# Replanning the instruction order of an attention and gated-convolution kernel, and moving part of the last batch's output behind its branch

## The chip, the cores and the metric

The kernel runs on one core of a Trainium2 chip. The metric is the device time of one execution in microseconds (us). An engine's program is a list of instructions that it takes strictly in order; engines wait for each other through semaphores. The names used here are those of the profile: PE is the matrix engine (PEld its weight loads), DVE the vector engine, ACT the scalar engine, POOL the GpSimd engine, SP the engine that issues most transfers.

## What is computed

For 8 batches, 12 heads, 448 positions and 64 channels a head:

```python
scores = scale * np.matmul(q, k.transpose(0, 1, 3, 2))
e = np.exp(scores - m)                       # m: row maximum
attn = e / (np.sum(e, -1, keepdims=True) + np.exp(-m) + 1e-09)
x = np.matmul(attn, v)                       # heads side by side: (8, 448, 768)
x1, x2, x3 = split(x @ w_proj, 3)            # w_proj: (768, 2304)
x2_conv = irfft(rfft(x2, axis=1) * rfft(filter_fft, axis=0), n=448, axis=1)
out = (x1 * x2_conv * x3) @ w_out            # (8, 448, 768), float32
```

## The kernel before, in words

The work of a batch has two halves. **Attention** runs over 6 pairs of heads (`attention(i)`, i from 0 to 47): PE makes scores (L817, L819), ACT exponentials (L830, L836), PE the product with v and the sums (L848, L856), DVE divides (L869 to L871) into the tile `xb`, which is turned into `xT` by PE (L953) or by a transposing transfer (L944). The exponentials are taken without the row maximum; the smallest denominators are collected in `low`, and at the end `watch()` makes a flag of them. **Dense** (`dense(b)`) folds `xT` on DVE (L1017, L1022), projects to x2 (`P`, L1045; `PS`, L1067, for batches 5 to 7), goes to the spectrum (`Z`, L1115 or L1119), multiplies it by the filter's on DVE (L1133, L1139), goes back (`I`, L1204), unfolds on DVE (L1222, L1224, L1233), makes the gates x1 and x3 (`G`, L1165, ACT L1177, DVE L1180), multiplies (L1248, tiles `yT` and `yR`), and projects out (`O`, L981), which ACT copies out of PSUM (L1279) and SP stores (L1286, L1289).

q, k and v come in float32. Those of batches 0 and 1 are staged (`staged`), and those of batches 2 to 7 loaded through rooms (`loaded`); SP issues the loads, and POOL casts them to bf16 (L468, L474, L481 and L597, L599, L613, L634, L646). The weights are loaded by POOL, which casts them on the way: the filter (L711 to L715), `wproj_bf` in four pieces (L795) and `wout_bf` (L800).

**The order is made by a planner.** `Plan.add` takes tasks: an engine, a cost in us, a wanted time, what it needs and makes, what buffers and PSUM banks it takes and gives back, and for a transfer its own duration (`dma`). `Plan.run` plays them through: whenever an engine is free it takes, among the first 160 of its tasks by wanted time, the first that is ready by the planner's own clock. The order found is then written out, and is fixed: on the chip an engine waits in that order. The wanted times come from lists of constants (`ATT`, `SLOT`, `LATER` for the pairs, `DENSE`, `PACE`, `FOLD`, `GATE`, `OUT` for the dense work, `LEAD`, `HOLD`, `EARLY1` for loads, `LOAD` for weights). They are priorities, and only an argument `after` forbids an earlier start; the weights' `LOAD` times are such bounds. `Plan.fillers` puts small matmuls on a tile of zeros (L1431) into the planned idle time of PE from 3 to 36 us.

**The end.** After `plan.run()` each engine loads the flag into a register (L1488) and compares (L1490). If a denominator was too small, the body of the branch does everything again in a stable way; with these inputs it isn't run. Tasks added with `keep=True` are not written out in their place but by `plan.rest()` (L1509), behind the branch, because the body would otherwise have to undo them. In the kernel before, these are the copies and stores of the last batch's output tiles of `st` 2 and 3 (four copies at L1279, three stores); all its matmuls and the copies of `st` 0 and 1 stand ahead of the branch:

```python
keep = b + 1 == n_batches and st > 1
```

The last batch takes its output tiles (st, ch) in the order (0,0), (0,1), (1,0), (1,1), (3,0), (3,1), (2,0), (2,1); the first three are multiplied in two parts (4 and 2 of the 6 matmuls).

Of the kernel before, what the change touches and what calls it, by code (L numbers as in the profile page):

```python
# [20 lines left out]
SP = 112  # L21
# [20 lines left out]
class Plan:  # L42
# [12 lines left out]
    DELAY = 0.8  # L55
    TURN_ISSUE, TURN_HOLD = 1.2, 0.3
    SHIFT = {}
    OPEN = 8
    BEGIN = 0.75

# [13 lines left out]
    def add(self, eng, cost, want, emit, need=(), make=(), take=(), give=(), dma=0.0, run=256, n=1, after=0.0, begun=(), late=0.0, turn=False, part=None, keep=False):  # L74
        want += self.SHIFT.get(part, 0.0)
        self.tasks.append((want, len(self.tasks), eng, cost, emit, need, make, take, give, dma, after, run, n, begun, late, turn, keep))

    def run(self):
# [14 lines left out]
        free = {e: self.BEGIN for e in queue}  # L93
        begin = {}
# [103 lines left out]
        while any(queue.values()):  # L198
            moved = False
            for e in queue:  # L200
# [18 lines left out]
                end = free[e] = now + t[3]  # L219
# [4 lines left out]
                if t[9]:  # L224
                    q = queues["POOL" if e == "POOL" else "SP"]
                    if t[15]:

                        begin[t[1]], free[e] = now, 1e9
                    q.append([now + 1.1 if t[15] else end + self.DELAY, t[9], t])
                    q.sort(key=lambda h: h[0])  # L230
                else:
                    done(t, end, e)
# [12 lines left out]
        for i, (_, t) in enumerate(order):  # L245
            if i in full:
                self.fill(*full[i])
            if t[16]:
                mine = {x for key in t[8] for x in self.banks.get(key, ())}
                assert not any(mine & {*self.banks.get(key, ())} for _, o in order[i:] for key in o[7])  # L250
                self.kept.append(t)
            else:
                t[4]()
# [30 lines left out]
def kernel(  # L284
# [14 lines left out]
    NSTAGED = 2  # L299
    TURNED = (5, 6, 7)  # L300
    SPIN = 38
    EARLY1 = -37.75
    ATT = [-28.66, -4.15, 82.66, 88.63, -11.62, 245.08, 188.29, 237.93]
    SLOT = [1.03, 11.04, 13.5, 24.02, 22.71, 6.32, -1.86, -14.05]
    LATER = [6.49, 7.1, 16.33, 26.04, 24.32, 5.99, -1.3, -2.41]
    GATE = [0.05, 3.09, 0.39, 0.33, 5.25, -4.56, -17.89, 14.82]
    OUT = [-3.82, -5.82, 1.94, 3.86, -0.16, 42.73, -1.71, 0.08]
    DENSE = [90.41, 90.02, 159.62, 189.84, 206.75, 232.76, 314.84, 367.32]
    PACE = [1.11, 3.24, 3.53, 2.89, 4.16, 2.12, 4.12, 4.66]
    FOLD = [-97.25, -48.09, -37.96, -86.97, -68.61, 36.98, -3.27, -113.82]  # L310
    BPS = -32.54
    RE1 = -1.35
    WT = -57.72
    FT = -26.69
    LEAD = [[-7.64, -155.36, 10.87, 83.2, 24.35, -314.59, 11.65], [-160.72, 35.85, -106.91, 64.9, -12.51, -20.99, -13.36], [-43.31, 108.31, -186.99, -24.09, -295.49, 10.18, 192.79], [-246.92, 212.51, -116.13, -76.77, -135.16, -81.28, 61.49], [-160.4, -105.54, 47.21, 18.57, 50.04, -291.15, -125.18], [-84.91, -13.51, -157.96, 191.73, -71.67, 188.48, 135.6]]
    LOADS = ((1, 0), (1, 1), ("F", None), (0, None), (2, None), ("O", None))
    LOAD = [8.53, 39.59, -42.24, 14.08, 48.04, 64.38]
    XALL = (1, 2, 3, 4, 5, 6, 7)
    HOLD = [16.92, -20.63]
    FOLD0 = [-27.94, 10.52, -65.43]  # L320
# [104 lines left out]
    def staged(b):  # L425
# [3 lines left out]
        for hp in range(NHP):  # L429
# [6 lines left out]
            for n, (name, x, at, size) in enumerate(parts):  # L436
                src = stage(g, at, size)

                def load(name=name, x=x, src=src, hp=hp, g=g):
# [13 lines left out]
                add("ACT" if first else "SP", 0.52 if first else 0.3, -21.0 if first else want + 0.1 * n, load, need=need,  # L453
                    make=[("s" + name, g)], after=hold, dma=(0.98 if name == "q" else 0.76) if b == 0 else 0.88 if name == "q" else 0.68, run=57,
                    begun=[("i" + name, g)])
                if hp == 0 and name != "q":
                    add("SP", 0.3, want + (0.05 if name == "k" else SLOT[0] + 0.05) if b == 0 else want - RE1 + 0.1 * n,
                        lambda name=name, x=x: nc.sync.dma_start(rests[:, "kv".index(name)], shared(x, b)),
                        need=[("cr" + name, b - 1)] if b else (), make=[("r" + name, b)],
                        dma=0.95, run=15, begun=[("ir", b)])  # L460
# [25 lines left out]
                if name == "v":  # L486
                    add("POOL", 0.72, tau(g) + (1.0 if b == 0 else -4.0), cast,
                        need=[("sv", g)] + ([("V", old, 1)] if b >= 2 else []), make=[("cv", g), ("v", g)])
                else:
                    add("POOL" if on_pool else "DVE", 0.65 if on_pool else 0.42, tau(g) - 5.0, cast,  # L490
                        need=[("s" + name, g)] + ([("c" + name, g - 1)] if g else []), make=[("c" + name, g)], take=[(name + "0", g)])
            if hp == 0:
                for u in range(2):
                    c = slice(64 * u, 64 * u + 64)
                    on_pool = b > 0 or u == 1
                    add("POOL" if on_pool else "DVE", 0.55 if on_pool else 0.37, tau(g) - 5.9 if g else 3.0,
                        lambda c=c, on_pool=on_pool: (nc.gpsimd if on_pool else nc.vector).tensor_copy(
# [71 lines left out]
    def loaded(b):  # L569
# [21 lines left out]
        for n, (name, x) in enumerate((("k", k), ("v", v))):  # L591
            add("SP", 0.3, tau(i0) - lead[0] - 0.2 + 0.1 * n,
                lambda name=name, x=x: nc.sync.dma_start(rests[:, "kv".index(name)], shared(x, b)),
                need=[("cr" + name, b - 1)], make=[("r" + name, b)], dma=0.85, run=15)
        for u in range(2):
            c = slice(64 * u, 64 * u + 64)
            add("POOL", 0.6, tau(i0) - lead[1] - 0.2, lambda c=c: nc.gpsimd.tensor_copy(kn[c, :, 0, c], rests[c, 0]),  # L597
                need=[("rk", b)] + (["zero kn"] if b == NSTAGED else [("kT", i) for i in range(i0 - NHP, i0)]), make=[("crk", b)])
        add("POOL", 0.56, tau(i0) - lead[3], lambda: nc.gpsimd.tensor_copy(vn[b % 2][:, :, 3, 0:DH], rests[:, 1]),  # L599
            need=[("rv", b), ("V", i0 - NHP - 1, 1)], make=[("crv", b), ("vr", b)])  # L600

        for hp in range(NHP):
# [3 lines left out]
            add("SP", 0.3, tau(g) - lead[4],  # L606
# [4 lines left out]
                need=[("cq", g - QS)] if n >= QS else staged_done, make=[("sq", g)], dma=0.88, run=57)  # L611
            add("POOL", 0.65, tau(g) - lead[5],
# [5 lines left out]
            if hp % few == 0:  # L618
                gs = range(g, g + few)
                add("SP", 1.3, tau(g) - lead[6], lambda hp=hp: q_turn(hp), need=[("cq", i) for i in gs] + [last],  # L620
                    make=[("qT", i) for i in gs], dma=(0.72, 1.9)[few > 1], run=11, late=-0.7, turn=True)
            for n, (name, x) in enumerate((("k", k), ("v", v))):
# [5 lines left out]
                add("SP", 0.3, tau(g) - lead[0] + 0.1 * n,  # L628
                    lambda x=x, hp=hp, src=src: nc.sync.dma_start(src.rearrange("p (u c) -> p u c", u=2), rows(x, b, hp)),
                    need=room, make=[("s" + name, g)], dma=0.68, run=57)  # L630
                sv = src.rearrange("p (u j d) -> p u j d", u=2, j=3)
                if name == "k":
                    add("POOL", 0.6, tau(g) - lead[1],
# [4 lines left out]
                    if hp % few == 0:  # L638
                        gs = range(g, g + few)
                        add("SP", 1.3, tau(g) - lead[2], lambda hp=hp: k_turn(hp), need=[("ck", i) for i in gs] + [("crk", b), last],  # L640
                            make=[("kT", i) for i in gs], dma=(0.97, 2.05)[few > 1], run=11, late=-0.7, turn=True)
                else:
# [5 lines left out]
                    add("POOL", 0.72, tau(g) - lead[3], cast, need=[("sv", g), ("V", g - 2 * NHP, 1)], make=[("cv", g), ("v", g)])  # L648
# [156 lines left out]
    def attention(i):  # L805
# [161 lines left out]
        if b in XALL or b > 1 and hp < NHP - 1:  # L967
            if hp in (2, NHP - 1 if b in XALL else NHP - 2):
                ps = range(0, 3) if hp == 2 else range(3, hp + 1)
                add("SP", 1.3, w, x_dma, need=[("xb", NHP * b + h) for h in ps] + old,  # L970
                    make=[m for h in ps for m in (("X", NHP * b + h), ("xT", b, h))], dma=(0.0, 1.1, 1.7, 2.1)[len(ps)], run=11, late=-0.7, turn=True)
# [17 lines left out]
    def dense(b, calm=True):  # L989
# [39 lines left out]
        for ds in (slice(0, 3), slice(3, 6)) if b else (slice(0, 3), slice(3, 4), slice(4, 6)):  # L1029
# [3 lines left out]
            for n in range(2):  # L1033
                add("DVE", (0.65, 0.54)[n] * slow, w, lambda ds=ds, n=n: first(ds, n),
                    need=[("xT", b, h) for h in range(ds.start, ds.stop)] + ([("fold", b, g, 0)] if n else []),
                    make=[("fold", b, g, n)], take=[("uw"[n], (b, g))])
                for pg in (2 * n, 2 * n + 1):
                    add("DVE", 0.26 * slow, w, lambda ds=ds, pg=pg: second(ds, pg),
# [51 lines left out]
        def PS(dt):  # L1090
# [7 lines left out]
            if dt % 3 == 2:  # L1098
                add("SP", 1.3, w - 2.0, lambda: turn2(ch), need=[("x2s", b, d) for d in range(dt - 2, dt + 1)],
                    make=[("x2", b, pg, ch) for pg in range(4)], take=[("x2", b)], give=[("x2s", b)],  # L1100
                    dma=2.1, run=11, late=-0.7, turn=True)
# [42 lines left out]
        def Z(par, ch):  # L1144
# [9 lines left out]
            for n in range(2):  # L1154
                tk = (f"t{n}", (b, par, ch))
                add("DVE", 0.48, w + 1.0, lambda n=n: product(par, ch, n),
                    need=[("xs", b, par, ch), ("hrs", par)], make=[("t", b, par, ch, n)],
                    take=[tk], give=[xs])
                add("DVE", 0.28, w + 1.5, lambda n=n: total(par, ch, n), need=[("t", b, par, ch, n)],
# [90 lines left out]
        def I(dt):  # L1250
# [9 lines left out]
            for n in range(2):  # L1260
                add("DVE", 0.32, w + 0.4, lambda n=n: halves(dp, n), need=[("cr", b, dp)], make=[("cw", b, dp)],
                    take=[cw], give=[cr])
            for n in range(2):
                add("DVE", 0.31, w + 0.5, lambda n=n: unfold(dp, n), need=[("cw", b, dp)], make=[("cv", b, dp)],
                    take=[cv], give=[cw])
            for n in range(2):
                add("DVE", (0.48, 0.15)[n], w + 1.0, lambda n=n: gated(dp, n), need=[("cv", b, dp), ("g", b, dp)],
# [23 lines left out]
        def O(st, ch):  # L1291
            hy, os_ = hold(("O", b, st, ch)), ("os", (b, st))
            keep = b + 1 == n_batches and st > 1
            if keep:
                plan.open.append((st, ch))
# [3 lines left out]
            if 2 * st + ch < 3:  # L1299
# [4 lines left out]
                    make=[("O", b, st, ch)], give=[mem_])  # L1304
            else:
                add("PE", 0.98, w, lambda: project(st, ch, None, hy), need=need + ["wout"], make=[("O", b, st, ch)],
                    take=[hy], give=[mem_])
# [232 lines left out]
```

## Time and profile before

| | |
|---|---|
| median of 3 runs (lowest, highest) | 390.51 us (389.07, 391.35) |
| the profiled execution, its own time | 387.02 us |
| its span, from first to last instruction | 385.2 us |
| granted clock of PE, mean | 0.997 |
| busy: PE, PEld, DVE, ACT, POOL | 364.6, 225.9, 262.2, 264.0, 114.2 us |
| PE: instructions | 3694 matmuls, as many weight loads |
| moved by DMA; read from and written to HBM | 66.82 MB; 43.86 and 11.01 MB |

The span leaves out 1.8 us that lie around the instructions. Busy time counts each moment once for an engine; PE's includes the small matmuls on zeros. The profile's groups give, for a line of the program, the engine, the operation, the tiles, how often, the busy time, the mean duration in ns, and the idle time of the engine just ahead with what ended it. An arrow `<-DVE xb L871` reads "released by that instruction".

### The profile page before, as it was taken

To read this page: it belongs to the slowest core of one execution; us is meant where nothing else is said; L and a number is where in the kernel's file an instruction comes from. 1 tells how busy PE (TensorE), PEld (TensorE's weight loads), DVE (VectorE), ACT (ScalarE), POOL (GpSimd) and SP (SyncE) were. 2 spreads that over 40 slices of the span, in tenths; PEclk is the share of its full clock that TensorE was granted. 3 is DMA by queue.
4 is the path that set the end of the run, shared out by engine and by line. 5 is a ranking of instruction groups with operands and counts; after the bars stand their busy time and mean duration, and the time that the engine had idled before them with its cause. 6 is when DMAs were issued, how large, how long until landed. Compare 5 with 4: busy or idle time off the path is not lost. (4 is left out here: it accounts for less than half of the span.)

```text
span 385.2 us, 9574 instructions
## 1 busy us (share of the span) xinstructions
PE 364.6 (95%) x3694; PEld 225.9 (59%) x3694; DVE 262.2 (68%) x677; ACT 264.0 (69%) x457; POOL 114.2 (30%) x240
## 2 busy tenths in 40 slices
PE   8888899999998999999998999999999999999992
PEld 6666575557664666556754675655555555555651
DVE  6484778875789547886599784675397833968650
ACT  6668776874877768778758468866788776446531
POOL 4925816030652445434367324110000000000000
PEclk9999999999999999999999999999999999999998
DMA  8999999977989699999998983594522164223214
GB/s 212 258 223 246 228 229 222 177 160 225 220 210 249 188 275 256 234 205 281 246 262 180 268 216 103 148 172 128 85 42 43 43 163 125 43 39 85 82 41 129
DMA packets 125744, 66.82 MB, mean 173 GB/s; under 512 B 82493, under 2 KB 122112, under 8 KB 125696
## 3 DMA queue, kind: packets, MB, share of 16 engines
q1 hardware_dynamic: 120976, 60.54, 67.6%
q0 software_dynamic: 4480, 5.41, 8.3%
q8 instruction: 30, 0.49, 0.5%
q10 hardware_dynamic: 240, 0.23, 0.2%
q14 instruction: 18, 0.15, 0.1%
HBM read 43.86 MB, written 11.01 MB: 142 GB/s over the span
## 5 line engine op out<-in xcount | busy, mean ns | idle before, releaser
L830 ACT ACTIVATE e<-psum 128x896 bf16<-128x896 f32 x144 | 127.1, 923 | 21.3 <-PE psum L817 20.8
L1165 PE MATMUL psum<-xT,wproj_bf 128*128 128x448 bf16 x576 | 121.4, 352 | 0.4 <-DVE g L1180 0.4
L1165 PEld LDWEIGHTS <-wproj_bf 128*128 128x128 bf16 x576 | 54.2, 97 | 45.2 <-issue 2.0
L981 PE MATMUL psum<-wout_bf,yT 128*128 128x384 bf16 x288 | 52.1, 326 | 0.0
L856 PE MATMUL psum<-vn,e 128*128 128x65 bf16 x1152 | 44.9, 194 | 0.0
L817 PE MATMUL psum<-qT,kT 64*128 64x448 bf16 x288 | 41.5, 355 | 3.2 <-DVE xb L871 2.1
L1045 PE MATMUL psum<-wproj_bf,xf 128*113 128x384 bf16 x240 | 43.1, 327 | 0.2 <-DVE xb L871 0.2
L1177 ACT CAST x<-psum 128x448 bf16<-128x448 f32 x48 | 25.7, 536 | 24.7 <-PE psum L1165 23.1
L856 PEld LDWEIGHTS <-e 128*128 128x128 bf16 x1152 | 40.2, 97 | 3.2
L1279 ACT COPY osb<-psum 128x384 f32<-128x384 f32 x56 | 25.7, 487 | 21.8 <-PE psum L981 18.0
L869 DVE TENSOR_SCALAR den<-psum 128x8 f32<-128x8 f32 x48 | 7.8, 162 | 48.2 <-PE psum L856 48.0
L1133 DVE TENSOR_TENSOR t<-xs,hrs 113x768 bf16<-113x768 bf16 (+1 forms) x64 | 36.8, 607 | 2.5 <-ACT xs L1127 2.4
L981 PEld LDWEIGHTS <-yT 128*128 128x128 bf16 x288 | 27.2, 98 | 18.9 <-issue 1.4
L613 POOL CAST nat<-nat 112x512 bf16<-112x512 f32 x36 | 26.9, 755 | 34.6 <-DMA nat<-in_q_dram 34.1
L1045 PEld LDWEIGHTS <-xf 128*113 128x113 bf16 x240 | 31.0, 132 | 8.8 <-issue 1.1
L871 DVE TENSOR_TENSOR xb<-psum,den 128x512 bf16<-128x512 f32 x48 | 33.2, 691 | 1.7
L1180 DVE TENSOR_TENSOR g<-x,psum 128x448 bf16<-128x448 bf16 x48 | 29.5, 615 | 6.0 <-PE psum L1165 6.0
L836 ACT ACTIVATE er<-psum 128x448 bf16<-128x448 f32 x48 | 26.3, 548 | 9.1 <-PE psum L819 9.1
L646 POOL CAST vn<-nat 128x192 bf16<-128x192 f32 x58 | 22.3, 408 | 34.2 <-DMA nat<-in_v_dram 18.0
L1127 ACT CAST xs<-psum 113x384 bf16<-113x384 f32 (+1 forms) x64 | 28.2, 497 | 5.4 <-PE psum L1119 2.1
L1213 ACT CAST cr<-psum 128x452 bf16<-128x452 f32 x48 | 25.0, 549 | 7.3 <-PE psum L1204 7.0
L817 PEld LDWEIGHTS <-kT 64*128 64x128 bf16 x288 | 9.1, 94 | 26.4 <-issue 23.9
(125 smaller groups left out, 474.5 us busy)
## 6 DMA issues: line engine op xcount, KB each, us to landing
nat<-in_q_dram SPq DMA_DIRECT2D x47, 224.0 KB, 4.5
out_dram<-osb SPq DMA_DIRECT2D x24, 384.0 KB, 3.0
nat<-in_k_dram SPq DMA_DIRECT2D x41, 192.0 KB, 4.3
nat<-in_v_dram SPq DMA_DIRECT2D x41, 192.0 KB, 4.6
wproj_bf<-in_moe_w_proj_dram POOLq DMA_DIRECT2D x2, 1152.0 KB, 15.0
rests<-in_k_dram SPq DMA_DIRECT2D x8, 192.0 KB, 5.1
rests<-in_v_dram SPq DMA_DIRECT2D x8, 192.0 KB, 5.0
out_dram<-osb SPq DMA_DIRECT2D x8, 192.0 KB, 3.1
```

Of the source, the lines that this page charges most:

```text
L613: lambda hp=hp, qsrc=qsrc: nc.gpsimd.tensor_copy(qn[:, hp].rearrange("p j (u d) -> p u j d", u=2), qsrc.rearrange("p (u j d) -> p u j d", ...
L817: nc.tensor.matmul(sc[:, u, 0:S], kT[b % 2][c, hp, t, :], qT[b % 2][c, hp, :])
L830: nc.scalar.activation(to, of, AF.Exp, scale=SCALE)
L836: nc.scalar.activation(to, of, AF.Exp, scale=SCALE)
L856: nc.tensor.matmul(out_bank(u)[:, n, :], P["e"][1 + t][:, u * S + n * 128 : u * S + n * 128 + 128], vn[b % 2][:, hp, 4 * u + t, :], start= ...
L871: nc.vector.tensor_tensor(W["xb", b][:, hp].rearrange("p n (u d) -> p u n d", u=2), op[:, :, :, 0:DH], rec[:].unsqueeze(3).to_broadcast([1 ...
L981: nc.tensor.matmul(ops[:n, :DCH], y[:, dt, 0:n], wout_bf[:, dt, ch * DCH : (ch + 1) * DCH], start=(dt == 0), stop=(dt == NDT - 1),)
L1045: nc.tensor.matmul(pps[:FQ, :DCH], W["xf", b][:, pg, kt, 0:FQ], wproj_bf[:, kt, D + ch * DCH : D + (ch + 1) * DCH], start=(kt == 0), stop= ...
L1127: nc.scalar.copy(L["xs", par, ch][:K, pg % 2, :], L["Z", pg, ch][:K, :DCH])
L1133: nc.vector.tensor_tensor(t[:K], L["xs", par, ch][:K], h, op=ALU.mult)
L1165: nc.tensor.matmul(p[:, :S], wproj_bf[:, kt, 2 * part * D + dt * 128 : 2 * part * D + (dt + 1) * 128], xT()[:, kt, 0:S], start=(kt == 0), ...
L1180: nc.vector.tensor_tensor(g[:, dt, :], L["x1", dt], p[:, :S], op=ALU.mult)
```

## The change

Three things are changed. None alters what is multiplied or how often, apart from the matmuls on zeros, whose number follows from the plan.

1. **The planner's model.** A shared port is added: a task with `port=True` (the bf16 sums and products on DVE: L1014 to L1022, L1133, L1139, L1222 to L1248, and the casts on DVE) and every task of POOL that isn't a transfer may not overlap by more than 0.16 us with one of the other engine. The casts on POOL get lower costs of their own. An issue on SP costs 0.5 instead of 0.3, and a transfer begins 1.15 (SP) or 1.9 us (POOL) after its issue starts. Durations and shares of transfers are changed a little.
2. **The constants** of the wanted times are all new, so that the whole order is new. Two pieces of `wproj_bf` get later bounds: the first half of the x2 part from 8.53 to 22.57, the x1 part from 14.08 to 21.47.
3. **The end.** All copies and stores of the last batch's output go behind the branch, and so do the matmuls of its tiles (1,1), (3,0), (3,1), (2,0), (2,1). Those of `TAIL` stay ahead of it. If the branch were taken, the body would multiply the `TAIL` tiles again.

```diff
-    DELAY = 0.8
-    TURN_ISSUE, TURN_HOLD = 1.2, 0.3
+    DELAY = (1.15, 1.9)
+    TURN_ISSUE, TURN_HOLD = 1.4, 0.4
+    PORT = 0.16
...
-                end = free[e] = now + t[3]
+                end = now + t[3]
+                if t[17]:
+                    end = max(now, port["POOL" if e == "DVE" else "DVE"] - self.PORT) + t[3]
+                    port[e] = end
+                free[e] = end
...
-                    q.append([now + 1.1 if t[15] else end + self.DELAY, t[9], t])
+                    q.append([now + self.DELAY[e == "POOL"], t[9], t])
...
+    TAIL = ((0, 0), (0, 1), (1, 0))
...
-    EARLY1 = -37.75
-    ATT = [-28.66, -4.15, 82.66, 88.63, -11.62, 245.08, 188.29, 237.93]
-    SLOT = [1.03, 11.04, 13.5, 24.02, 22.71, 6.32, -1.86, -14.05]
-    LATER = [6.49, 7.1, 16.33, 26.04, 24.32, 5.99, -1.3, -2.41]
...
-    DENSE = [90.41, 90.02, 159.62, 189.84, 206.75, 232.76, 314.84, 367.32]
+    EARLY1 = -43.88
+    ATT = [-15.23, -18.02, 73.57, 108.86, 36.32, 226.98, 200.24, 223.07]
+    SLOT = [8.8, 12.52, 11.4, 17.9, 3.71, 0.09, -13.77, -15.9]
+    LATER = [5.59, 20.08, 17.05, 19.3, 12.65, -6.44, -8.83, 0.12]
...
+    DENSE = [84.12, 91.93, 155.59, 189.18, 196.52, 273.03, 309.83, 339.74]
...
     LOADS = ((1, 0), (1, 1), ("F", None), (0, None), (2, None), ("O", None))
-    LOAD = [8.53, 39.59, -42.24, 14.08, 48.04, 64.38]
+    LOAD = [22.57, 41.98, -44.36, 21.47, 43.35, 63.54]
...
-                add("SP", 0.3, tau(g) - lead[0] + 0.1 * n,
+                add("SP", 0.5, tau(g) - lead[0] + 0.1 * n,
...
-                    add("POOL", 0.6, tau(g) - lead[1],
+                    add("POOL", 0.47, tau(g) - lead[1],
...
-                add("DVE", 0.48, w + 1.0, lambda n=n: product(par, ch, n),
+                add("DVE", 0.48, w + 1.0, lambda n=n: product(par, ch, n), port=True,
...
-            keep = b + 1 == n_batches and st > 1
-            if keep:
+            keep = b + 1 == n_batches
+            last = keep and (st, ch) not in TAIL
+            if keep and not last:
                 plan.open.append((st, ch))
...
-                    take=[hy], give=[mem_])
+                    take=[hy], give=[mem_], keep=last)
             add("ACT", 0.38, w, lambda: project_back(st, ch), need=[("O", b, st, ch)], make=[("os", b, st)],
                 take=[os_], give=[hy], keep=keep)
...
+        y, yr = W["yT", n_batches - 1], W["yR", (n_batches - 1) // 2]
         W.clear()
         main = plan
         for b in range(n_batches):
+            W["yT", b], W["yR", b // 2] = y, yr
```

## The prediction on record

> **What bounds the kernel now.** I read the page's busy times and slices first, then stretches of the span, then the pauses of PE, then the end in order of time.
>
> ```profile
> PE 364.6 (95%) x3694; PEld 225.9 (59%) x3694; DVE 262.2 (68%) x677; ACT 264.0 (69%) x457; POOL 114.2 (30%) x240
> ...
> PE   8888899999998999999998999999999999999992
> ```
>
> PE is the bound: busy 95%, and in the slices short only in the first four or five and in the last. So the change can gain in three places alone: the start, the few pauses between, the end. The stretches say how much lies in each.
>
> ```profile
> 7.75:40.00 32.25, 26.80 (x418) 19.54 (x418) 18.43 (x53) 23.73 (x38) 19.88 (x50) 1.00 1.15 244
> ...
> 40.00:370.00 330.00, 322.87 (x3144) 195.48 (x3144) 236.33 (x598) 232.86 (x406) 91.19 (x179) 1.00 0.75 169
> ```
>
> After the time, the columns are PE, PEld, DVE, ACT, POOL. **Start:** 7.75 us is where the first exponential begins. PE looks busy for 26.80 of 32.25 us, but 7.03 are matmuls on zeros (L1431 in the same stretch), so it works some 19.8. ACT idles 32.25 - 23.73 = 8.5 us; attention, all that PE has there, can't pass it. **Middle:** PE idles 330 - 322.87 = 7.1 us. From 280 to 320 and 330 to 370 it doesn't pause.
>
> **Part 1, casts and products apart.** The group of L1233 in two windows, 40 to 260 us (POOL casts) and 260 to 386 (POOL does next to nothing):
>
> ```profile
> L871 DVE TENSOR_TENSOR xb<-psum,den 128x512 bf16<-128x512 f32 x30 | 20.7, 691 | 1.0
> ...
> L1233 DVE TENSOR_TENSOR cv<-cw 128x448 bf16<-128x448 bf16 x30 | 13.1, 474 | 0.5
> ```
>
> ```profile
> L871 DVE TENSOR_TENSOR xb<-psum,den 128x512 bf16<-128x512 f32 x12 | 8.3, 691 | 0.4
> L1233 DVE TENSOR_TENSOR cv<-cw 128x448 bf16<-128x448 bf16 x18 | 6.2, 388 | 0.3
> ```
>
> The bf16 sum takes 474 ns beside casts and 388 without; the product out of PSUM takes 691 in both. So what the planner now keeps apart does collide. The same difference over the other bf16 forms of 40 to 260 us: L1233 30 x 86 = 2.6 us, L1133 20 x 107 + 20 x 69 = 3.5, L1139 20 x 89 + 20 x 87 = 3.5, L1022 18 x 83 + 18 x 28 = 2.0, L1248 15 x 31 + 14 x 95 = 1.8, L1222 15 x 51 = 0.8: 14.2 us of DVE. But DVE idles a third of the span, so this counts only where PE waits for it. One such place, in order of time:
>
> ```profile
> 207.15 0.87 DVE L1233 TENSOR_TENSOR cv<-cw 128x448 bf16<-128x448 bf16 x2
> ...
> 207.66 1.39 POOL L613 CAST nat<-nat 112x512 bf16<-112x512 f32 x2 [0.18 <-DMA nat<-in_q_dram]
> ...
> 208.05 0.51 DVE L1248 TENSOR_TENSOR yR<-g,cv 128x128 bf16<-128x128 bf16 x1
> ...
> 208.91 0.69 DVE L871 TENSOR_TENSOR xb<-psum,den 128x512 bf16<-128x512 f32 x1
> ...
> 209.66 0.37 PE L1204 MATMUL psum<-bt,yh 113*128 113x113 bf16 x4 [1.41 <-DVE xb L871]
> ```
>
> Beside POOL's casts the small product takes 0.51 us (220 ns without casts), the division behind it is late, and PE waits 1.41 for it. PE's longer pauses after 40 us (from one matmul's start to the next, less the usual spacing) sum to 9.0; three have a product drawn out by a cast ahead of them, at 161.9, 195.9 and 207.9 us: 0.58 + 0.99 + 1.58 = 3.15. Four more (81.9, 123.3, 124.5, 233.3: 0.90 + 0.80 + 0.57 + 1.08) are mostly the order's own, scores put right behind the matmuls whose division frees their banks. A new order can lose as much as it wins in such places: between a loss of 3 and a gain of 3.15 + half of 3.35 I take a gain of **1.3**, some 40% of what the collisions cost.
>
> Longer issues on SP (0.5 for 0.3) alter the plan alone: load issues on the chip take 0.37 to 0.46 us at the least and in the median (L446). Casts on POOL average 570 (L634) and 755 ns (L613) with collisions, so 0.47 and 0.58 beside a port are no gain in themselves. I put both at nothing, behind 70% idle POOL; if the cover is gone, they show as waits of PE on casts, in the range.
>
> **Part 2, the start.** Weights now come no earlier than 21.47 and 22.57 in planned time, where POOL issued them at 15.15 and 16.57. From 20 to 30 us POOL's queue moved 1.47 MB and SP's 0.72, so the weights slow the loads of batches 0 and 1: q, k, v issued then landed after 10 to 13 us, against 4.3 to 4.6 over the whole run. The filter, which isn't moved, fills POOL's queue until about 19 us, and the weights flow from 20. With about 2 us from issue to first packet they would flow from 23.4: 3.4 us in which SP's queue gets some 230 KB/us instead of 75, or 0.5 MB, which is two or three loads. The two pieces are 1152 + 576 KB, at 147 KB/us 11.8 us, landed by about 35; the first use of the x2 part is at 42.4 (L1045). So they are still in time. What is late next is ACT: it also makes the filter's copies there (29.05 to 33.96 us, 4.2 us of work), so pair 5 starts at 33.87 whatever the loads do. Of ACT's 8.5 us the named waits on PE are nearly all; recovering 2 us of ACT gives PE 2 x 19.8 / 23.73 = 1.7. Bounds: a loss of 5.0 (late weights, below), a gain of half of the 8.5, 4.2 x 0.83 = 3.5. I take a gain of **1.5**.
>
> **Part 3, the end.** Before:
>
> ```profile
> 376.34 2.11 PE L981 MATMUL psum<-wout_bf,yT 128*128 128x384 bf16 x12
> 378.63 1.63 ACT L1279 COPY osb<-psum 128x384 f32<-128x384 f32 x4 [3.56 <-PEq L1490]
> 379.51 1.12 SPq L1289 DMA_DIRECT2D out_dram<-osb  x2
> 380.75 0.52 SPq L1286 DMA_DIRECT2D out_dram<-osb  x1
> ```
>
> Four copies and three issues stand behind PE's end: its last matmul starts at 378.13, the last store is issued at 380.75, 2.62 us later. After, seven copies (0.37 us apart) run beside the 30 matmuls behind the branch (30 x 0.162 = 4.9 us), and only one is left when PE ends. By the unhindered tile at 372.97, a copy starts 0.04 behind its last matmul's end: 0.33 + 0.04 + 0.49 + 0.02 = 0.88 to the store. Gain 2.62 - 0.88 = 1.74. What it adds is a stop of PE in the middle of its output tiles:
>
> ```profile
> L1488 PEldq TENSOR_LOAD <-flag x1: 488/488/488, 375.4 to 375.4; - x1
> ...
> L1490 PEldq COMPARE_BRANCH  x1: 488/488/488, 376.0 to 376.0; - x1
> ...
> L1490 PEldq EVENT_SEMAPHORE  x1: 51/51/51, 378.5 to 378.5; - x1
> ```
>
> PE's sequencer reads the flag and branches while some 2.7 us of matmuls are still queued, and the semaphore step behind the branch waits for the last of them (378.45). The next matmul could start at about 378.8 instead of 0.162 behind the last, 378.29: 0.5 lost. Bounds: 0.3 (semaphore at once) and 3.1 (375.4 to 378.5, nothing hidden). Queued behind it are 30 matmuls, and all copies and stores wait for them; SP no longer waits at the branch for the output stores (it did, until 377.84), which wins nothing as PE was last. Net **1.2**; the last store, alone in the queues, may also land up to 0.5 earlier (2.74 against 3.26 us), which I leave in the range.
>
> A rule speaks against this part: the Trainium skill (Runtime: NRT & Kernel Launch, Instruction fetch mechanics) says that a taken branch to a target outside the fetched window stalls until a page is fetched. Here PE stood behind the branch at 376.47 and was ready by 378.50, so the row allows up to 2.0 us of fetch, which the queue of matmuls hid; by the row I charge 0.5, by the rule unhidden 3.1.
>
> **Sum:** 1.3 + 1.5 + 1.2 = 4.0 us. Against the profiled execution 387.02 - 4.0 = 383.0. The runs shown have a median 3.5 us above it; the same gain from 390.51 gives **386.5**.
>
> **Rivals.**
> - Only the end counts: the new order makes as many pauses as it removes. For it: every wait of an in-order engine that goes uncovers another. 390.51 - 1.2 = 389.3. 0.14.
> - More comes out: half of ACT's idle start (3.5), all collisions (3.15), the end with its landing (1.6), 8.25 in all: 382.3. For it: PE never pauses after 280 us, so all won earlier is kept. 0.16.
> - The fetch isn't hidden: 3.1 lost instead of 0.5, 386.5 + 2.6 = 389.1. Against it: in the rows above the branch ran ahead. 0.06.
> - Slower: the weights come late. If they move only as POOL's queue did from 10 to 20 us (0.72 MB in 10 us), 1.73 MB take 24 us from 23.4 on and land at 47.4, and the x2 projection of batch 0 starts 5.0 later than 42.4; it decides as soon as they land past 42.4 with no attention left to fill PE. 390.51 + 5.0 - 1.2 - 1.3 = 393.0. Against it: 7 us of margin. 0.16.
> - That the order isn't changed can't be: the wanted times decide it.
>
> **Chances.** The forecast itself 0.48, with 383.5 to 388.5 as its own range. A measurement of this kernel can tell about 0.5% (2 us) from no change. Faster: the forecast and "more", 0.64; within: "only the end" and the fetch, 0.20; slower: late weights, 0.16. The range 381.0 to 391.5 leaves out the late weights and reaches, below, 1.3 past "more" for a better middle.
>
> **What would show it.** After: PE's matmuls behind 36 us without zeros, batch 0's sixth division before 39.3, L1045's first matmul by 42; L1233 near 400 ns while POOL casts; the last store issued 0.9 us behind the last matmul's start, and PE's stop at L1490 of 0.3 to 0.7 us. Wrong would be: L1045 waiting for `wproj_bf`, new pauses of PE over 1 us between 40 and 280, or a stop of 2 us or more at the branch.

## The result, and the profile after

| | before | after |
|---|---|---|
| median of 4 runs each (lowest, highest) | 390.21 us (389.07, 391.35) | 384.77 us (383.79, 385.54) |
| ratio after / before, 95% interval | | 0.9859 [0.9822, 0.9897] |
| profiled execution, its own time | 387.02 us | 383.79 us |
| its span | 385.2 us | 378.4 us |
| around the span | 1.8 us | 5.4 us |

The kernel became 5.4 us faster (1.4%). Two things in the table pull against each other: in the profiled executions the span shrank by 6.8 us, more than the time, and 3.6 us came back outside it. In this document medians and spans are of all executions of a kernel, while ratios leave out those more than 1.5% above its quickest, so that the two can differ.

The page of the changed kernel, parts 1 and 2:

```profile
PE 366.7 (97%) x3675; PEld 226.4 (60%) x3675; DVE 260.2 (69%) x677; ACT 263.8 (70%) x457; POOL 110.8 (29%) x240
...
PE   8889999999999999999999999999999999999995
...
PEclk9989999999999999999999999999999999999999
```

PE is still the bound, and its last short slice is now half full (5 for 2). New is the 8 in the third slice of the granted clock. The same two stretches as before, of the changed kernel (after the time: PE, PEld, DVE, ACT, POOL, granted clock, DMA share, GB/s):

```profile
7.75:40.00 32.25, 28.40 (x412) 19.87 (x410) 19.12 (x56) 23.07 (x36) 20.82 (x52) 0.95 1.15 249
40.00:370.00 330.00, 327.33 (x3170) 197.45 (x3170) 236.34 (x601) 233.83 (x410) 86.85 (x177) 1.00 0.76 169
```

**Middle:** PE is busy 327.33 instead of 322.87 us: 4.46 us gained. **Start:** PE is busy 28.40 instead of 26.80 us, 6.82 of it with zeros (7.03 before), but the clock is 0.95: 0.05 x 32.25 = 1.6 us of PE's capacity is lost. Nothing is gained: counting the matmuls that are not zeros, each by its usual spacing, PE is at 40 us where it was before, to within 0.2 us. **End:** from the last matmul's start to the span's end 7.09 before, 4.42 after; PE's block of output matmuls is 0.30 longer; net 2.37. The three sum to the 6.8 by which the span shrank.

Where the middle's gain lies shows in the waits of PE from 40 to 370 us, before:

```profile
PE psum L817 <- DVE xb L871: 2.1, 3, 0.9
PE psum L1204 <- DVE xb L871: 1.4, 1, 1.4
PE psum L1119 <- DVE x L1057: 1.1, 2, 0.8
PE psum L817 <- DVE kT L527: 0.9, 1, 0.9
```

and after (the same lines lie 6 further down):

```profile
PE psum L823 <- DMA kT<-nat: 0.7, 1, 0.7
PE psum L1171 <- DVE xb L877: 0.6, 1, 0.6
PE psum L987 <- DVE yT L1254: 0.3, 1, 0.3
PE psum L1125 <- DVE x L1063: 0.3, 1, 0.3
```

The columns are total, times, longest. All the waits listed for this stretch fall from 6.9 us to 2.3, about the 4.46 gained; those for the division `xb` fall from 3.7 to 0.8 (over the whole span from 7.3 to 1.9). The longest waits left are at the start, for POOL's cast of `q`:

```profile
PE psum L523 <- POOL q L481: 2.4, 3, 1.5
```

The collisions changed little. The two groups from 40 to 260 us, after:

```profile
L877 DVE TENSOR_TENSOR xb<-psum,den 128x512 bf16<-128x512 f32 x31 | 21.4, 691 | 1.1
L1239 DVE TENSOR_TENSOR cv<-cw 128x448 bf16<-128x448 bf16 x30 | 11.8, 430 | 0.5
```

The small sum takes 430 ns instead of 474, half way to the undisturbed 388. Over all bf16 products of this stretch, what they take beyond the 20th percentile of their form sums to 16.9 us before and 14.7 after; 58 of 229 before and 53 of 236 after lie more than 50 ns above it, and are called lengthened here. The planner keeps casts and products apart in its own clock; on the chip no semaphore does.

The end, after (timeline; the last columns are the idle time and its releaser):

```profile
366.07 4.37 PE L987 MATMUL psum<-wout_bf,yT 128*128 128x384 bf16 x24
...
369.27 0.78 PEld L987 LDWEIGHTS <-yT 128*128 128x128 bf16 x6 [0.51 <-issue]
369.33 1.63 ACT L1285 COPY osb<-psum 128x384 f32<-128x384 f32 x4 [3.62 <-PEq L1497]
...
374.38 0.48 ACT L1285 COPY osb<-psum 128x384 f32<-128x384 f32 x1 [0.45 <-PE psum L987]
374.88 0.34 SPq L1292 DMA_DIRECT2D out_dram<-osb  x1
```

One copy instead of four stands behind PE's end. The last matmul starts at 374.01, the last store is issued 0.87 later (2.62 before), and it lands at 377.21, 2.33 behind its issue (3.26 before). PE's branch:

```profile
L1497 PEldq COMPARE_BRANCH  x1: 388/388/388, 368.2 to 368.2; - x1
...
L1497 PEldq EVENT_SEMAPHORE  x1: 51/51/51, 369.2 to 369.2; - x1
```

It cost PE a gap of 0.47 us, 0.3 more than the usual spacing.

**What came back.** Past the span's end at 378.4, from 379 to 384 us, the changed kernel's trace holds only this:

```profile
q14 instruction: 4, 0.03, 2.1%
q8 instruction: 1, 0.02, 1.2%
```

Five fetches of instructions (four of 8 KB, one of 16 KB), between 381.2 and 382.6, after the last instruction of the program. All four runs of the changed kernel have 4.6 to 5.4 us around their span; the 71 runs of the kernel before that stand beside the experiments all have 1.8 or 1.9.

### The profile page after: what moved, and what is told of

It reads as the page before. It is cut to its first block, busy times and chain, and to the rows that moved or that the text cites. A ratio compares the mean times of both kernels' runs of the same rounds, so it can differ in the third digit from the quotient of the medians.

```text
span 378.4 us, 9534 instructions
## 1 busy us (share of the span) xinstructions
PE 366.7 (97%) x3675; PEld 226.4 (60%) x3675; DVE 260.2 (69%) x677; ACT 263.8 (70%) x457; POOL 110.8 (29%) x240
## 5 line engine op out<-in xcount | busy, mean ns | idle before, releaser
L823 PE MATMUL psum<-qT,kT 64*128 64x448 bf16 x288 | 42.7, 358 | 0.8 <-DMA kT<-nat 0.7
L619 POOL CAST nat<-nat 112x512 bf16<-112x512 f32 x36 | 24.5, 685 | 52.8 <-DMA nat<-in_q_dram 49.3
L1139 DVE TENSOR_TENSOR t<-xs,hrs 113x768 bf16<-113x768 bf16 (+1 forms) x64 | 35.3, 585 | 4.1 <-ACT xs L1133 3.9
L1133 ACT CAST xs<-psum 113x384 bf16<-113x384 f32 (+1 forms) x64 | 28.0, 495 | 4.5 <-PE psum L1121 2.4
L652 POOL CAST vn<-nat 128x192 bf16<-128x192 f32 x58 | 21.5, 396 | 25.1 <-DMA nat<-in_v_dram 15.6
```

What stands on the lines that cost most here:

```text
L823: nc.tensor.matmul(sc[:, u, 0:S], kT[b % 2][c, hp, t, :], qT[b % 2][c, hp, :])
L1133: nc.scalar.copy(L["xs", par, ch][:K, pg % 2, :], L["Z", pg, ch][:K, :DCH])
L1139: nc.vector.tensor_tensor(t[:K], L["xs", par, ch][:K], h, op=ALU.mult)
```

## The experiments

Three questions stand behind them. Does the end bring what its rows say, or does PE's stop or a fetch eat it? Is the middle's gain that of products kept out of POOL's way, or that of an order whose constants happen to fit one plan? And what became of the start: was it the clock that held it back?

**The end alone**, on the kernel before:

```diff
+    TAIL = ((0, 0), (0, 1), (1, 0))
-            keep = b + 1 == n_batches and st > 1
-            if keep:
+            keep = b + 1 == n_batches
+            last = keep and (st, ch) not in TAIL
+            if keep and not last:
```

(with `keep=last` on the matmuls, as in the change.)

> The kernel before with only the change at its end: copies and stores of the last batch's output and the matmuls of five of its tiles behind the branch, order and constants of before. Theory A (the gain is two separate parts, 4.4 us won by the order between 40 and 260 us and the rest at the end): the last matmul comes 0.3 to 0.6 us later than before (378.4 to 378.7 instead of 378.1), from its start to the end of the span 4.4 instead of 7.1 us, so the span is 2.0 to 2.4 us shorter and the time about 388.0 beside 390.2. Theory B (the branch fetch is hidden only with the new order): PE stops 2 to 3 us at the branch, the time is 389.5 to 391. By the prediction's own term: 1.2 us faster.

Measured: 387.2 us (384.27 to 389.71, 12 runs) beside 388.97 (35 runs), ratio 0.996 [0.9923, 0.9996]; median span 1.75 less. Its trace has the changed kernel's end exactly; in the timeline one copy stands behind PE,

```profile
381.54 0.48 ACT L1280 COPY osb<-psum 128x384 f32<-128x384 f32 x1 [0.45 <-PE psum L982]
382.05 0.34 SPq L1287 DMA_DIRECT2D out_dram<-osb  x1
```

4.42 us from the last matmul's start to the span's end, PE's block 0.31 longer, and 1.8 us around the span. So part 3 does what was said of it, by itself, and it is not what brings the fetches at the end.

**The new order alone**, the end as before:

```diff
-            keep = b + 1 == n_batches
-            last = keep and (st, ch) not in TAIL
-            if keep and not last:
+            keep = b + 1 == n_batches and st > 1
+            last = False
+            if keep:
```

> The changed kernel with the end as before (copies and stores of tiles st 2 and 3 behind the branch, all matmuls ahead of it); model, constants and order of the changed kernel. Theory A: the order keeps its 4.4 us and the end gives back 2.0 to 2.4, so the time is about 386.9, 3.2 below before. Theory C (the order's gain is mostly gone without the end, since what is won earlier waits at the branch): 389 or more. Prediction's terms: 2.8 us faster than before.

Measured: 389.82 (384.38 to 392.49, 12 runs) beside 388.97, ratio 0.9965 [0.992, 1.0009]; median span 1.35 less. A miss: 386.9 had been expected. Eight of the 12 executions have some 5.2 us around the span, and the end is not that of before. PE's branch, and behind it the timeline:

```profile
L1497 PEldq COMPARE_BRANCH  x1: 3622/3622/3622, 374.9 to 374.9; - x1
...
L1497 PEldq EVENT_SEMAPHORE  x1: 51/51/51, 378.5 to 378.5; - x1
```

```profile
375.23 2.11 PE L987 MATMUL psum<-wout_bf,yT 128*128 128x384 bf16 x12
378.68 1.63 ACT L1285 COPY osb<-psum 128x384 f32<-128x384 f32 x4 [4.72 <-PEq L1497]
```

PE's branch took 3.62 us instead of 0.49, with instruction fetches running from 375.9 to 377.2 us; the four copies wait for it though PE is done, and the end is 8.63 us long instead of 7.09. The Trainium skill (Runtime: NRT & Kernel Launch, Instruction fetch mechanics) says that a taken branch out of the fetched window stalls for a page. This row fits that; the changed kernel's 388 ns show no such stall. The profiled execution also lost clock twice (mean 0.986), and it is the only one of the twelve that was traced, so whether the others stall at the branch is not known. The run doesn't price the order alone.

**Casts doubled**, on the kernel before and on the changed one: each cast of v on POOL is made twice, to the same place, so that POOL meets more products, and nothing else changes.

```diff
+                            for _ in range(2):
                                 nc.gpsimd.tensor_copy(
                                     vn[b % 2][:, hp, 4 * u : 4 * u + 3, 0:DH], sv[:, u]
                                 )
```

> The kernel before with each of the 96 casts of v on POOL done twice into the same place: POOL has some 36 us more of work, the same order, and the bf16 products on DVE collide more often. If collisions with casts are what makes PE pause in the middle (theory P), the products' lengthening between 40 and 260 us rises from 17 to 22 us or more and PE's work done by 260 us falls behind by 1 to 3 us: time 391.5 to 393. If they hardly matter there (theory S: the gain is a better fitted order, not fewer collisions), the lengthening rises all the same and the time stays within 1 us, 389.5 to 391.

> The changed kernel with each cast of v on POOL done twice, order unchanged. Theory P (the new order wins because casts and products lie apart): putting collisions back gives up a good part of its gain, 386.5 to 389. Theory S (its gain doesn't hang on collisions): 384.5 to 386, no more than 1 us above the changed kernel.

Measured: on the kernel before 389.02 (10 runs), ratio 1.0011 [0.9974, 1.0047], although 81 products instead of 58 were lengthened and the sum beyond the percentile is 19.8 us instead of 16.9: more collisions cost the kernel before nothing that can be measured. (That does not show that the collisions it has cost nothing.) On the changed kernel 386.43 (10 runs), ratio 0.9943 [0.9912, 0.9975], 75 lengthened, with 18.9 us beyond the percentile; the span keeps 2.5 us of the gain, so some 4 are lost. That speaks for collisions there, but the casts themselves also take longer, and the profile has two windows at half clock (as has that of the unaltered kernel measured again below, with a span of 381.7 us against 384.4 here): this half doesn't decide.

**The planner's port off**, with the new constants:

```diff
-... keep, port or eng == "POOL" and not dma))
+... keep, False))
```

> The changed kernel, constants and all other costs the same, but the planner doesn't know the shared port (no task counts as using it); the order that comes out is another. Theory P (knowing the port is what makes the order good): collisions rise (products between 40 and 260 us lengthened by 18 us or more, against 14.7 in the changed kernel) and the middle's gain of 4.4 us goes: about 388 to 390. Theory S (the constants were fitted to one plan, and any other plan from them is worse): slower by about as much as the kernel with a neutral nudge of the planner that runs beside it, with no clear rise of the collisions.

**Two controls**: an order drawn anew by a nudge to the model that has nothing to do with the port (PE's latency 0.21 for 0.20; issues on SP at 0.45 for 0.5).

```diff
-    LAT = {"PE": 0.2, "ACT": 0.22,
+    LAT = {"PE": 0.21, "ACT": 0.22,
```

```diff
-            add("SP", 0.5,
+            add("SP", 0.45,
```

> A control: the changed kernel with the planner's delay behind PE at 0.21 instead of 0.20 us, all else the same. No theory gives this a meaning of its own; what it costs is what any re-drawn order from these constants costs. Theory P: within 1 us of the changed kernel, 384 to 386. Theory S: 1 to 4 us slower, 386 to 389.

> A second control: the changed kernel with an issue on SP at 0.45 instead of 0.50 us in the planner. Theory P: within 1 us of the changed kernel, 384 to 386. Theory S: 1 to 4 us slower, 386 to 389.

**The old constants** in the changed model, with the new end (all lists of wanted times as before):

```diff
-    ATT = [-15.23, -18.02, 73.57, 108.86, 36.32, 226.98, 200.24, 223.07]
+    ATT = [-28.66, -4.15, 82.66, 88.63, -11.62, 245.08, 188.29, 237.93]
...
-    LOAD = [22.57, 41.98, -44.36, 21.47, 43.35, 63.54]
+    LOAD = [8.53, 39.59, -42.24, 14.08, 48.04, 64.38]
```

> The changed kernel's planner model (port, casts, issues) and end with the wanted times of before. If the model alone makes a better order from any constants (theory P): 390.2 less 2.2 for the end, less 1 to 3 for the model, 385 to 387. If constants and model only work as a fitted pair (theory S): the order is no better than before, 388 or more, the end's 2.2 us or less being all that is left.

Measured on one chip, beside 390.15 (25 runs):

| kernel | median, us (runs) | ratio | median span, us | beyond the percentile, us |
|---|---|---|---|---|
| port off | 392.87 (10) | 0.9958 [0.9894, 1.0022] | +2.9 | 16.6 |
| latency nudged | 389.9 (10) | 1.0021 [0.9987, 1.0054] | -0.1 | 17.1 |
| issue nudged | 389.42 (10) | 0.9951 [0.9911, 0.9992] | -0.6 | 18.8 |
| old constants | 401.72 (4) | 1.031 [1.0243, 1.0376] | +11.7 | 17.2 |

The ratio of "port off" rests on 2 of its 10 runs. All four carry the new end, worth 1.75 to 2.4 us, and no median span is shorter than before by that much: of the order's gain nothing is left. Taking the port away loses it, as the collision theory wanted, but without the rise in collisions that it wanted with it (16.6 us, where 18 or more were expected); nudging PE's latency by 10 ns loses it as well. The old constants were expected at "388 or more" and are far worse than that. What differs is which waits of PE the order holds, with the port off (this trace is of the longest of its ten executions)

```profile
PE psum L1210 <- DVE g L1186: 5.3, 2, 4.0
PE psum L959 <- DVE xb L877: 4.3, 3, 2.6
```

with the latency nudged

```profile
PE psum L1171 <- DMA xT<-xb: 3.0, 2, 2.8
```

and with the old constants

```profile
PE psum L1171 <- DMA xT<-xb: 5.2, 3, 3.6
PE psum L959 <- DVE xb L877: 3.5, 4, 2.1
```

From 40 to 370 us PE's listed waits sum to 9.3 to 16.2 us in the traces of these four orders. In those of the old order they sum to 6.9 (before) and 8.9 (the end alone), in those of the changed order to 2.3 (after), 3.9 (the same kernel again, below) and 5.1 (the order alone). So the changed order has the fewer waits in every trace, but by how much hangs on the pair of traces: from 1.8 to 6.6 us.

The wanted times belong to one model and to one plan. The port's model has no effect that these runs, with one order drawn for each setting, can separate from drawing another order.

**The clock.** The changed kernel's third slice, in windows of 3.41 us whose edges are those of the clock's steps:

```profile
20.16:23.57 3.41, 1.56 (x20) 0.86 (x17) 3.19 (x8) 0.48 (x1) 2.97 (x5) 1.00 1.16 266
23.57:26.99 3.42, 3.42 (x43) 2.23 (x42) 1.76 (x4) 2.31 (x3) 3.42 (x9) 0.50 1.16 199
26.99:30.40 3.41, 3.41 (x62) 2.53 (x60) 2.86 (x9) 3.03 (x4) 1.93 (x5) 1.00 1.14 234
```

A window in which PE is busy 1.56 us (46%) is followed by one at half clock. Most of its idle time is the wait for POOL:

```profile
21.80 0.37 PE L523 MATMUL psum<-ident_bf,q 112*128 112x112 bf16 x4 [1.46 <-POOL q L481]
```

Is the start's missing gain in this window? Four kernels ran on one chip beside 389.84 (11 runs). The changed kernel unaltered:

> The changed kernel itself once more, beside the kernel before on one chip, to have many executions of both. Its four runs so far had 4.6 to 5.4 us around the span where the kernel before had 1.8. If that belongs to those executions and not to the kernel, its time is about 1.8 above its span and 381 to 383 in the median, some 6 to 7 below before. If it belongs to the kernel, the time stays 5.4 below before.

Zeros in all of PE's planned idle time to 36 us, instead of 0.6 of it:

```diff
-    FILL = (3.0, 36.0, 0.6)
+    FILL = (3.0, 36.0, 1.0)
```

> The changed kernel, order unchanged, with matmuls on zeros for all of the planned idle time of PE from 3 to 36 us instead of 0.6 of it. Clock theory (after a 3.4 us window in which PE is busy for less than about half, the granted clock is halved for the next; seen in all the profiles so far): some fewer halvings, mean granted clock 0.996 or more, time 0.5 to 1.5 us below the changed kernel beside it. Rival (the halving early is idle time of PE anyway, ACT being the bound there): same time within 0.5 us, or slower by the zeros' own time, up to 1 us.

24 zeros ahead of the turn that waits for `q`, and 24 more before one transpose of `xb` (fixed in place, not planned):

```diff
+                    for _ in range(24 if g == 4 else 0):
+                        nc.tensor.matmul(bank(("hy", ("T", g)))[:, 256:384], idle, idle)
...
+            for _ in range(24 if i == 3 else 0):
+                nc.tensor.matmul(bank(("hy", ("X", i)))[:, 256:384], idle, idle)
```

> The changed kernel, order unchanged, with 24 matmuls on zeros (24 x 0.056 = 1.3 us) in each of its two longest pauses of PE: between the transposes of k and q of pair 4 (PE waited 1.46 us at 20.3 us for the cast of q) and ahead of the transposes of xb of pair 3 (1.05 us at 31.5). Clock theory: no window below half is left, the granted clock is 1.0 up to the end in nearly every run, the time is 1 to 1.5 us below the changed kernel and its spread narrows. Rival: same time within 0.5 us.

No zeros from the planner at all:

```diff
-    FILL = (3.0, 36.0, 0.6)
+    FILL = (3.0, 36.0, 0.0)
```

> The changed kernel, order unchanged, without the matmuls on zeros that stand in the planned idle time of PE (the 38 at the very start stay). Clock theory: PE is busy for less than half in most windows up to 36 us, so the clock is halved in four or more of them (mean granted clock below 0.985), and every halving that meets work costs up to 1.7 us: 3 to 8 us slower than the changed kernel. Rival: the halved clock meets idle time and costs nothing, within 1 us.

| kernel | median, us (lowest, highest; runs) | ratio | median span, us |
|---|---|---|---|
| changed, again | 386.73 (381.6, 389.14; 6) | 0.9883 [0.9815, 0.995] | 381.6 |
| more zeros | 383.32 (382.15, 385.99; 6) | 0.9839 [0.9799, 0.9879] | 379.4 |
| zeros in pauses | 387.67 (380.08, 390.49; 6) | 0.9865 [0.9791, 0.9939] | 383.0 |
| no zeros | 382.01 (379.26, 389.6; 4) | 0.9788 [0.9715, 0.986] | 377.6 |

The changed kernel repeats a gain, 3.1 us between the medians and 6.4 between the median spans. Two of its executions have 1.8 us around the span and four 5.5 to 5.9, so neither of the two expectations holds for all of them. With more zeros no execution's clock fell below 0.997, and the median span is 2.2 us less, somewhat over one halved window (half of 3.41); but the first four executions of the unaltered kernel had 379.7 as well, so this doesn't settle what a halved window costs. The start gains nothing at full clock: from 7.75 to 40 us PE is busy 30.23 us, of which 10.61 are zeros, which leaves 19.62 of work against 19.77 in the kernel before. The traced execution with zeros in pauses, also at full clock, is no more than 0.2 us ahead of the kernel before at 40 us, counted by spacing. Zeros in two pauses gave full clock and 378.3 and 380.4 us of span in two executions, and 382.4 to 384.7 at a lower clock in the other four: inconclusive, since most of its executions still lost clock. The last kernel is a clear miss of both theories, which had it 3 to 8 us slower or the same. Without zeros the clock does fall,

```profile
7.75:40.00 32.25, 27.65 (x349) 17.77 (x348) 21.19 (x59) 26.29 (x43) 21.99 (x54) 0.89 1.15 263
```

to 0.89 at the start, and yet by 40 us PE is some 3 us of real matmuls ahead of the kernel before, and ACT does 26.29 us of work there where the changed kernel does 23.07. Zeros stand in PE's queue in order, and one place shows what that does. In both traces DVE has cast the first `k` by 5.06 us. PE turns it in the changed kernel behind 15 zeros,

```profile
5.14 1.66 PE L1438 MATMUL psum<-idle 128*128 128x128 bf16 x15
6.64 0.33 PE L516 MATMUL psum<-ident_bf,k 128*128 128x128 bf16 x3
```

and without them at once:

```profile
5.14 0.48 PE L516 MATMUL psum<-ident_bf,k 128*128 128x128 bf16 x3
```

The first exponential starts at 9.08 and 7.75 us. (In the traced execution with zeros in pauses the same 15 zeros took 1.00 us, and it starts at 7.95, so this price varies.) How the rest of the 3 us comes about was not followed. The kernel without zeros is the fastest version measured here: its interval against the kernel before is clear of 1. Against the changed kernel on the same chip its runs overlap (4 against 6), so that lead is likely and not settled.

The longer time around the span appears in 4 of these 6 runs of the unaltered changed kernel. Its traced execution has 1.8 us there, and no fetch behind its end, from 382.5 to 387.5 us:

```profile
DMA packets 0, 0.00 MB, mean 0 GB/s; under 512 B 0, under 2 KB 0, under 8 KB 0
```

The longer time also appears with more zeros (5 of 6), in pauses (3 of 6), with no zeros (3 of 4) and with the order alone (8 of 12), and never in the end alone, the doubled casts, the port off, the nudges or the old constants. Of all the traces, the four with 4.8 us or more around their span have the five fetches behind it, and the ten with 1.8 have none. So they go with the instruction streams of the changed plan; zeros added to PE's or taken from it leave them, and doubled casts, which alter POOL's alone, end them. Why is open.

## Why the prediction was right, and where it was not

Forecast 386.5, measured 384.77: right in sign and inside its range, though the terms were not. That the number came so near is in part luck. Between the two profiled executions the middle brought 3.2 us more than forecast, the start 1.5 less and the end 1.2 more, and 3.6 us around the span, which the sum didn't have, took the surplus away again.

- **PE is the bound, and only three places can gain:** right. All of the span's 6.8 us lie in two of them.
- **Collisions and middle, 1.3:** the step that failed. It came out at 4.46, and the reason given, that the order takes products out of POOL's way, is not borne out: collisions went down by 2.2 us of DVE work only, the forecast 400 ns for L1233 was 430, and raising them on the kernel before cost nothing that could be measured. Whether the three places that the prediction named were cured by fewer collisions or by other neighbours in the order, no run separates. What was mis-sized is the step "a new order can lose as much as it wins": from 40 to 370 us this order has PE's waits at 2.3 us instead of 6.9, and its pauses over 0.3 us after 40 us sum to less than 4 instead of 9.0. The controls show the other side: three orders drawn anew from the same constants (port off and the two nudges) give none of it, so the sign could not be read from the diff.
- **Start, 1.5:** wrong, it gave nothing. The markers were plain: batch 0's sixth division at 39.5 (39.3 before), L1045's first matmul at 42.5 (42.4 before). The weights were in time, and no wait for `wproj_bf` appeared, so the cover held. The transfers moved as forecast: from 20 to 30 us SP's queue carried 1.45 MB instead of 0.72. But the loads of q, k and v issued there still took about 12 us to land, and the step that failed is "recovering 2 us of ACT": ACT worked 23.07 us up to 40 instead of 23.73. PE lost a halved window to a new wait for POOL's cast, though without that window the start gains nothing either; and, as the run without zeros shows, its queue of zeros holds back what comes early.
- **End, 1.2:** the mechanism right, in every row: 0.87 us from the last matmul's start to the store (0.88 forecast), PE's stop 0.3 (0.5 charged, bounds 0.3 to 3.1). The mis-sized term is the landing of a store that is alone: 0.93 us less, where up to 0.5 was left to the range. 1.75 + 0.93 - 0.3 = 2.4. The rival "the fetch isn't hidden" did not occur in the changed kernel's trace, but it did, with 3.62 us, in that of the order alone.
- **Time against span:** the sum took the 1.8 us around the span as fixed. They became 5.4. So a span 6.8 shorter gave 3.2 between the two profiled executions. Between the medians the spans differ more, by 8.7 us (390.21 less 1.8 against 379.7), since the kernel before was profiled in an execution quicker than any of the four; less the 3.3 more around the median span that is the 5.4 measured.

"Only the end counts" (389.3) and "late weights" (393.0) are out by the result; "more comes out" (382.3) had its size in the span, but its reasons, the start and the collisions, did not hold.

What stays open: how much of the middle is the lengthening of products in the changed order (its doubled casts lose some 4 us of span), the price of the new order by itself, what the end's branch costs it, and why the fetches behind the end follow the streams.

## What to carry to other kernels

A hand-ordered kernel's gain from a new order can't be read from the costs that the planner was taught: count the waits of the engine that bounds, by what they wait for, before and after, and run a nudged order as a control before crediting a cause. Copies and stores that stand behind the last matmul can be brought beside matmuls: here that was worth 1.75 to 2.4 us, and the last store, now alone, landed 0.93 us sooner. Dummy work in an in-order queue can delay real work by more than it helps; try the kernel without it.

## What the runs showed of the hardware

- **The clock falls after a pause far shorter than a window.** In these profiles it steps in windows of 3.41 us. From 5 us to the kernels' ends, all windows at full clock in which PE was busy 14 to 45% were followed by one at half clock, and none of 57% and more. Between them it went both ways: 46% here (1.56 of 3.41 us, with a pause of 1.46) and 55% with the port off (from 27.9 us) were followed by half clock, while 46% without zeros (from 121.5 us) and with the old constants (from 130.2 us) were not. So it turns at about half, but not sharply, and not "in all the profiles". The Trainium skill (TensorE: Matmul & The Clock Gate, Part 1: The HAM clock gate) gives a free-running window of 3413 ns, and has the clock fall after an idle window. The steps here agree with its length; half an idle window was enough. The windows lie differently in the traces, which may be part of the spread of single executions.
- **Time can lie behind a program's last instruction.** In the profiled execution it was 3.6 us more than in the kernel before, and the trace holds nothing there but five instruction fetches; that they are what takes the time is inferred. It came in most executions of some kernels and in none of others. A span alone would have told 6.8 us of gain where 3.2 arrived.
- **The same branch took 0.39 us on PE in the changed kernel and 3.62 in one trace of its order alone**, the latter with instruction fetches under way.
- **The small bf16 sum** takes 430 to 474 ns on the mean in the stretch of POOL's casts instead of 388, and the product that reads PSUM 691 in either. With DVE busy 68%, 23 more lengthened products moved no time in the kernel before.
